# Cosformer attention with a quick-GELU feed-forward: the last block's stores issued by SyncE in place of GpSimd

## The chip, the cores and the metric

The kernel runs on one core of a Trainium2 chip. The metric is device time in microseconds (us) of one execution. Before the change the median of three runs is 294.02 us (294.0 to 294.31). The engines are named as in the profile: PE is TensorE's matmul, PEld its weight load, DVE is VectorE, ACT is ScalarE, POOL is GpSimd and SP is SyncE. A "q" behind an engine's name (SPq, POOLq) marks an instruction that its sequencer handles by itself: a semaphore wait, a drain, the issue of a transfer.

## The reference

Eight batches, eight heads, 576 positions, head size 64. A linear attention with cosine and sine weights gives an array of 4608 tokens by 512, and a feed-forward layer of width 2048 with the sigmoid form of GELU follows:

```python
q_p = phi(q, cos_w, sin_w)            # relu(x)*cos, relu(x)*sin, side by side
k_p = phi(k, cos_w, sin_w)
kv = np.einsum('bhsf,bhsd->bhfd', k_p, v)
num = np.einsum('bhsf,bhfd->bhsd', q_p, kv)
den = np.einsum('bhsf,bhf->bhs', q_p, np.sum(k_p, axis=2))[..., None] + 1e-06
x = (num / den).transpose(0, 2, 1, 3).reshape(4608, 512)
h = x @ w_in                          # 512 -> 2048
out = (h * (1.0 / (1.0 + np.exp(-1.702 * h)))) @ w_out   # 2048 -> 512, f32
```

## The kernel before

A block is one batch. Of its 576 tokens, 512 are worked on as four tiles of 128 (`t` = 0 to 3); the 64 that are left are a tail, and the tails of two batches make one more tile (`t` = 4). The order of the instructions is written out by hand, and every engine takes its own in that order.

In each block PE multiplies the block's x by `w_in` (`mm1`, L279), ACT applies the GELU (L284), and PE multiplies the result by `w_out` (`mm2`, L328). Between the parts of `mm2`, the attention of the next batch is done (L214, L227, and DVE at L235 to L239), and SP issues the transposing transfers that bring it into place (L268). The inputs of later blocks are loaded by transfers on SP's queue.

`mm2` is the function to follow. When the sum over the 16 pieces of `w_out` is complete, ACT copies the result from its accumulator into an SBUF tile `ysb` (L332; the pool has four such tiles), and for every piece of rows that `rows` names one transfer to `out` is issued (L335). In all blocks these stores are issued on POOL's queue, with one exception, the second half of the very last tile, which SP issues.

The last block (`b` = 7, `nb` is None) has no next batch to prepare. It does its `mm1`, then the first product of all tails that are left (`mm1_tails`, L307), then `mm2` for three tail tiles (two stores of 64 rows each), then `mm2` for the tiles 0 to 2 (one store of 128 rows each), and then the last tile in two halves of 256 columns, so that the final copy and the final store are small.

DMA completions are counted by semaphores. Each queue has eight that its transfers take in turn, and a transfer waits until the one before it on the same semaphore has landed. At the very end (the launch line, L538) SP waits for all of these semaphores, two to an instruction, in nine instructions. Then there is a barrier: every engine executes a drain instruction and then counts up one semaphore; POOL, after its own drain, waits for the four others and releases them all; POOL clears the semaphores; and the barrier is gone through a second time.

Of the kernel before, what the change touches and what calls it, by code (L numbers as in the profile page):

```python
# [19 lines left out]
def kernel(  # L20
# [9 lines left out]
    nc = tc.nc  # L30
    B, H, S, D = q.shape
    d_model = H * D
    d_ff = moe_w_in.shape[1]
    KC = d_model // 128
    FC = d_ff // 128
# [91 lines left out]
    def load_next(b):  # L127

        load_q(b, nc.sync)
        load(kf, k, b, nc.sync)  # L130
        load(vf, v, b, nc.sync)
# [14 lines left out]
    def trig(dst, src, j, act=False):  # L146
        i = src[:, :, ts(j, 64)]
        for cs, w in enumerate((cosw, sinw)):
            o = dst[:, j, :, ts(cs, 64)]
            if act:  # L150
                nc.scalar.activation(o, i, AF.Relu, scale=w[:, j:j + 1])
            else:
                nc.vector.tensor_scalar(o, i, 0.0, w[:, j:j + 1], op0=MAX, op1=MUL)  # L153

    def trig_q(c, act=False):
        n = 128 if c < 4 else 64
        if c < 4:
            i = qf[:, 0:2048].rearrange("p (h c d) -> p c h d", h=H, c=4)[:, c]
        else:
            i = qf[0:64, 2048:2560].rearrange("p (h d) -> p h d", h=H)  # L160
        for cs, w in enumerate((cosw, sinw)):
            o, sc = qn[0:n, c, :, ts(cs, 64)], w[0:n, NS + c:NS + c + 1]
            if act:
                nc.scalar.activation(o, i, AF.Relu, scale=sc)
            else:
                nc.vector.tensor_scalar(o, i, 0.0, sc, op0=MAX, op1=MUL)  # L166

    def vcopy(i0, i1, act=False):
        o = vt[:, :, i0:i1, 0:64].rearrange("p j i e -> p i j e")
        i = vf[:, i0:i1].rearrange("p i (j e) -> p i j e", e=64)  # L170
        if act:
            nc.scalar.activation(o, i, AF.Copy)
        else:
            nc.vector.tensor_copy(o, i)  # L174
# [19 lines left out]
    def qturn_dma(c):  # L194
        n = 128 if c < 4 else 64
        nc.sync.dma_start_transpose(out=qT[:, :, c * 128:c * 128 + n],
                                    in_=qn[0:n, c].rearrange("p h f -> p (h f)"))
# [3 lines left out]
    def kv_open(i0=0, i1=NI):  # L201
        t = pat.tile([128, 2, 512], F32, name="at")
        for i in range(i0, i1):
            st["kv", i] = t[:, :, ds((i - i0) * 65, 65)]
        st["ps", i0] = t[:, :, 0:(i1 - i0) * 65]
        if i0 == 0:
            st["kvs"] = small.tile([128, 2, NI, VW], BF16, name="kvs", bufs=2)

    def kv_mm(i0, i1, rhs, col, n):
        for i in range(i0, i1):  # L210
            for j in range(NS):
                for hh in range(2):
                    r = slice(hh * 64, hh * 64 + 64)
                    nc.tensor.matmul(st["kv", i][:, hh, ds(col, n)], kr[r, j, i, :], rhs(r, i, j),  # L214
                                     start=(j == 0), stop=(j == NS - 1))

    def kv_evac(i0, i1):
        o = st["kvs"][:, :, i0:i1, 0:65]
        nc.vector.tensor_copy(o, st["ps", i0].rearrange("p hh (i e) -> p hh i e", e=65))  # L219
# [3 lines left out]
    def num_mm(c):  # L223
        ps = pat.tile([128, 2, 512], F32, name="at")
        for h in range(H):
            i, hh = divmod(h, 2)
            nc.tensor.matmul(ps[:, h // 4, ds((h % 4) * 65, 65)], qT[:, h, ts(c, 128)],  # L227
                             st["kvs"][:, hh, i, 0:65], start=True, stop=True)
        nums[c] = [ps]

    def num_div(c):
        ps = nums[c][0]
        pv = ps[:, :, 0:260].rearrange("p a (h e) -> p a h e", h=4)
        den = small.tile([128, 2, 4], F32, name="den")
        nc.vector.tensor_scalar(den, pv[:, :, :, 64], 1e-6, None, op0=ADD)  # L235
        inv = small.tile([128, 2, 4], F32, name="inv")
        nc.vector.reciprocal(inv, den)  # L237
        xn = small.tile([128, 2, 4, 64], BF16, name="xn", bufs=4)
        nc.vector.tensor_tensor(xn, pv[:, :, :, 0:64],  # L239
                                inv.unsqueeze(3).to_broadcast([128, 2, 4, 64]), op=MUL)  # L240
        nums[c].append(xn)
# [3 lines left out]
    def x_open(b):  # L245
        x[b] = xpool.tile([128, KC, MT], BF16, name="xT")
# [40 lines left out]
    def mm1(b, fc):  # L287
        mm1_part(b, fc, 0, MT)
        gelu(fc)
# [6 lines left out]
    def mm1_tail_first(b, half):  # L296
        hps = pmm.tile([128, 8, 64], F32, name="mm")
        for f in range(8):
            for kc in range(KC):
                nc.tensor.matmul(hps[:, f], wcol(kc, half * 8 + f), xt[:, kc, ts(b, 64)],  # L300
                                 start=(kc == 0), stop=(kc == KC - 1))
        nc.scalar.activation(gt[:, ts(half, 8), ts(b, 64)], hps, AF.Gelu_apprx_sigmoid)

    def mm1_tails(fc):
        hps = pmm.tile([128, MT], F32, name="mm")
        for kc in range(KC):
            nc.tensor.matmul(hps[:, 128:B * 64], wcol(kc, fc), xt[:, kc, 128:B * 64],  # L307
                             start=(kc == 0), stop=(kc == KC - 1))
        nc.scalar.activation(gt[:, fc, 128:B * 64], hps[:, 128:B * 64], AF.Gelu_apprx_sigmoid)
# [4 lines left out]
    def rows(b, t):  # L314

        if t == 4:
            return [(64 * u, 64, out_j[NS - 1] if b + u == 1 else out[(b + u) * S - 64:(b + u) * S])
                    for u in range(2)]
        if b == 0:
            return [(64 * u, 64, out_j[2 * t + u]) for u in range(2)]  # L320
        return [(0, 128, out[b * S:b * S + 512].rearrange("(p c) d -> c p d", c=4)[t])]

    def mm2(b, t, lo, hi, c0=0, c1=d_model, last=False):
        if lo == 0:
            yp[b, t, c0] = pmm.tile([128, d_model], F32, name="mm")
        for fc in range(lo, hi):
            w = gT[fc][:, ts(t, 128)] if t < 4 else gt[:, fc, ts(b // 2, 128)]
            nc.tensor.matmul(yp[b, t, c0][:, c0:c1], w, w_out_sb[:, fc, c0:c1],  # L328
                             start=(fc == 0), stop=(fc == FC - 1))
        if hi == FC:  # L330
            ysb = ypool.tile([128, d_model], F32, name="ysb")
            nc.scalar.activation(ysb[:, c0:c1], yp[b, t, c0][:, c0:c1], AF.Identity)  # L332
            for p0, n, dst in rows(b, t):
                eng = nc.sync if last else nc.gpsimd
                eng.dma_start(out=dst[:, c0:c1], in_=ysb[p0:p0 + n, c0:c1])  # L335

    def idle(n, cols=512):
# [100 lines left out]
    for g in range(2):  # L438
        for t in range(4):
            mm2(0, t, 4 * g, 4 * g + 4)  # L440
    mm2(0, 0, 8, 12)
    mm2(0, 1, 8, 12)
    kv_open()
    kv_mm(0, 4, vt_rhs, 0, 65)
# [21 lines left out]
    for b in range(1, B):  # L466
        nb = b + 1 if b + 1 < B else None
        f0 = 5 if b == 1 else 0
        for fc in range(f0, FC):
            if nb is not None and fc == f0:  # L470
                for c in range(5):
                    trig_q(c)
                    qturn_dma(c)
            if nb is not None and fc == f0 + 1:
                for j in range(NS):
                    trig(kr, kf, j)
                vcopy(0, 4)
                if nb + 1 < B:
                    load_next(nb + 1)
            mm1(b, fc)  # L480
        if nb is not None:
            x_open(nb)
        if b == 1:
            mm1_tail_first(1, 0)
            mm1_tail_first(1, 1)
        if nb is not None:
            kv_open()
            kv_mm(0, 4, vt_rhs, 0, 65)
            kv_evac(0, 4)
        if b == 1:  # L490
            mm2(1, 4, 0, FC)
        if nb is None:
            for fc in range(FC):
                mm1_tails(fc)
            for u in range(3, B, 2):
                mm2(u, 4, 0, FC)
        for t in range(4):
            last = nb is None and t == 3
            if last:
                mm2(b, t, 0, FC, 0, 256)  # L500
                mm2(b, t, 0, FC, 256, 512, last=True)
                continue
            mm2(b, t, 0, 8)
            if nb is not None and t < 3:
                num_mm(2 * t)
                num_div(2 * t)
                xturn_dma(nb, 2 * t)
            mm2(b, t, 8, 16)
            if nb is not None and t < 2:
                num_mm(2 * t + 1)  # L510
                num_div(2 * t + 1)
                xturn_dma(nb, 2 * t + 1)
# [30 lines left out]
```

## Time and profile before

| What | us |
|---|---|
| median of three runs | 294.02 |
| the profiled execution's own time | 294.29 |
| its span, first to last instruction | 292.6 |
| PE busy | 284.0 (97%) |
| ACT busy / DVE busy / POOL busy | 128.7 / 123.6 / 57.5 |
| last matmul ends about | 287.5 |
| last copy into `ysb` (ACT) | 287.59 to 287.97 |
| last store, issued by SP | 288.0, landing 1.9 later |
| granted TensorE clock, mean | 0.998 |

The span is counted from the first instruction to the last one, and the execution's own time is 1.7 us longer. Starts are microseconds from the span's start. Where the profile gives "x3: 51/102/5292", those are the shortest, the median and the longest duration, in nanoseconds, of three instructions. "To landing" is the time from the issue of a transfer until its semaphore is counted up.

### The profile page before, as it was taken

What the parts mean: (1) busy time and instruction counts of PE and PEld (TensorE: products, weight loads), DVE (VectorE), ACT (ScalarE), POOL (GpSimd) and SP (SyncE); (2) the same over time, 40 slices, a digit from 0 to 9 for tenths busy, and PEclk for the clock granted to TensorE, in tenths of its full rate; (3) what the DMA queues carried; (4) which work ended last, traced back from release to release, by engine and by line L of the source; (5) the groups of instructions that cost most, each with busy time, mean ns of one, the idle gap of its engine ahead of it and who ended that gap; (6) DMA issues with size and microseconds to landing.
All of it is one profiled execution on the core that took longest, in us unless ns stands there. A gap on an engine that the chain in (4) does not pass through costs nothing.

```text
span 292.6 us, 6031 instructions
## 1 busy us (share of the span) xinstructions
PE 284.0 (97%) x2461; PEld 157.6 (54%) x2461; DVE 123.6 (42%) x355; ACT 128.7 (44%) x224; POOL 57.5 (20%) x70
## 2 busy tenths in 40 slices
PE   8979999999999999999999999999999999999993
PEld 3775646857545554555555554555455545564452
DVE  4774415881478047903691269225931510000000
ACT  7947733663116611562146304631464136771111
POOL 6350003200216001600061014201330110001211
PEclk9999999999999999999999999999999999999999
DMA  7999999999989964999598859895840430001311
GB/s 252 240 224 286 347 179 238 370 205 245 382 161 182 303 248 116 176 249 312 136 176 243 306 142 166 208 357 137 152 99 2 104 97 25 1 0 38 72 72 72
DMA packets 72731, 53.54 MB, mean 183 GB/s; under 512 B 52608, under 2 KB 62464, under 8 KB 72704
## 3 DMA queue, kind: packets, MB, share of 16 engines
q1 hardware_dynamic: 66160, 35.53, 49.6%
q0 software_dynamic: 6544, 17.63, 22.5%
q8 instruction: 19, 0.31, 0.4%
q14 instruction: 8, 0.07, 0.1%
HBM read 36.70 MB, written 9.44 MB: 158 GB/s over the span
## 4 chain that ended last, share of the span: by engine, by line
PE 93%; DMA 4%; DVE 1%; POOL 0%; issue 0%; ACT 0%; ACTq 0%
PE mm L328 43%; PE mm L279 38%; PE mm L307 4%; PE at L227 3%; PE at L214 3%; DMA vb<-in_v_dram 2%; PE mm L300 1%; DMA kf<-in_k_dram 1%; PE at L256 1%; DVE xn L239 1%; POOL vb L139 0%; DVE inv L237 0%; PE mm L182 0%; DVE den L235 0%; ACT ysb L332 0%
## 5 line engine op out<-in xcount | busy, mean ns | idle before, releaser
L328 PE MATMUL mm<-w_out_sb,g 128*128 128x512 bf16 (+1 forms) x528 | 117.4, 372 | 0.0
L279 PE MATMUL mm<-xT,w_in 128*128 128x512 bf16 (+1 forms) x608 | 113.5, 345 | 0.0
L284 ACT ACTIVATE g<-mm 128x512 bf16<-128x512 f32 x128 | 75.6, 598 | 32.0 <-PE mm L279 31.9
L335 POOL DMA_DIRECT2D out_dram<-ysb x44 | 46.4, 1057 | 216.8 <-ACT ysb L332 216.7
L279 PEld LDWEIGHTS <-w_in 128*128 128x128 bf16 x608 | 61.7, 113 | 49.1
L328 PEld LDWEIGHTS <-g 128*128 128x128 bf16 x528 | 48.8, 98 | 50.0
L332 ACT ACTIVATE ysb<-mm 128x512 f32<-128x512 f32 (+1 forms) x37 | 21.7, 586 | 115.8 <-PE mm L328 115.8
L219 DVE CAST kvs<-at 128x520 bf16<-128x520 f32 (+1 forms) x9 | 5.8, 642 | 56.4 <-PE at L214 56.4
L239 DVE TENSOR_TENSOR xn<-at,inv 128x512 bf16<-128x512 f32 x40 | 27.6, 691 | 1.4
L153 DVE TENSOR_SCALAR kr<-kf,cosw 128x256 bf16<-128x256 f32 x68 | 23.3, 343 | 9.1 <-DMA kf<-in_k_dram 9.1
L153 DVE TENSOR_SCALAR kr<-kf,sinw 128x256 bf16<-128x256 f32 x68 | 23.5, 346 | 0.0
L235 DVE TENSOR_SCALAR den<-at 128x8 f32<-128x8 f32 x40 | 6.6, 166 | 37.1 <-PE at L227 37.1
L227 PEld LDWEIGHTS <-qT 128*128 128x128 bf16 x320 | 14.5, 97 | 7.3
L166 DVE TENSOR_SCALAR qn<-qf,cosw 128x512 bf16<-128x512 f32 (+1 forms) x33 | 15.7, 477 | 3.8 <-DMA qf<-in_q_dram 3.8
L227 PE MATMUL at<-kvs,qT 128*128 128x65 bf16 x320 | 15.9, 193 | 0.0
L166 DVE TENSOR_SCALAR qn<-qf,sinw 128x512 bf16<-128x512 f32 (+1 forms) x33 | 15.8, 477 | 0.0
L328 PE MATMUL mm<-w_out_sb,gt 128*128 128x512 bf16 x64 | 14.2, 379 | 0.0
L214 PEld LDWEIGHTS <-kr 64*128 64x128 bf16 x648 | 10.3, 94 | 4.0 <-issue 3.1
L307 PE MATMUL mm<-xt,w_in 128*128 128x384 bf16 x64 | 10.6, 326 | 0.0
L328 PEld LDWEIGHTS <-gt 128*128 128x128 bf16 x64 | 6.2, 97 | 7.3
L174 DVE CAST vt<-vf 128x2304 bf16<-128x2304 f32 (+1 forms) x7 | 8.9, 1264 | 0.6 <-DMA vf<-in_v_dram 0.6
L307 PEld LDWEIGHTS <-w_in 128*128 128x128 bf16 x64 | 7.2, 113 | 3.3
(57 smaller groups left out, 101.5 us busy)
## 6 DMA issues: line engine op xcount, KB each, us to landing
kf<-in_k_dram SPq DMA_DIRECT2D x6, 1152.0 KB, 9.4
vf<-in_v_dram SPq DMA_DIRECT2D x6, 1152.0 KB, 12.3
out_dram<-ysb POOLq DMA_DIRECT2D x27, 256.0 KB, 2.7
qf<-in_q_dram SPq DMA_DIRECT2D x6, 1024.0 KB, 6.9
out_dram<-ysb POOLq DMA_DIRECT2D x17, 128.0 KB, 6.1
w_out_sb<-in_moe_w_out_dram POOLq DMA_DIRECT2D x4, 512.0 KB, 18.1
kf<-in_k_dram POOLq DMA_DIRECT2D x1, 1152.0 KB, 12.3
vf<-in_v_dram POOLq DMA_DIRECT2D x1, 1152.0 KB, 20.6
```

The costliest lines, as they stand in the source:

```text
L153: nc.vector.tensor_scalar(o, i, 0.0, w[:, j:j + 1], op0=MAX, op1=MUL)
L166: nc.vector.tensor_scalar(o, i, 0.0, sc, op0=MAX, op1=MUL)
L174: nc.vector.tensor_copy(o, i)
L214: nc.tensor.matmul(st["kv", i][:, hh, ds(col, n)], kr[r, j, i, :], rhs(r, i, j), start=(j == 0), stop=(j == NS - 1))
L227: nc.tensor.matmul(ps[:, h // 4, ds((h % 4) * 65, 65)], qT[:, h, ts(c, 128)], st["kvs"][:, hh, i, 0:65], start=True, stop=True)
L239: nc.vector.tensor_tensor(xn, pv[:, :, :, 0:64], inv.unsqueeze(3).to_broadcast([128, 2, 4, 64]), op=MUL)
L279: nc.tensor.matmul(hp[fc][:, t0:t1], wcol(kc, fc), x[b][:, kc, t0:t1], start=(kc == 0), stop=(kc == KC - 1))
L284: nc.scalar.activation(g, hp.pop(fc), AF.Gelu_apprx_sigmoid)
L307: nc.tensor.matmul(hps[:, 128:B * 64], wcol(kc, fc), xt[:, kc, 128:B * 64], start=(kc == 0), stop=(kc == KC - 1))
L328: nc.tensor.matmul(yp[b, t, c0][:, c0:c1], w, w_out_sb[:, fc, c0:c1], start=(fc == 0), stop=(fc == FC - 1))
L332: nc.scalar.activation(ysb[:, c0:c1], yp[b, t, c0][:, c0:c1], AF.Identity)
L335: eng.dma_start(out=dst[:, c0:c1], in_=ysb[p0:p0 + n, c0:c1])
```

## The change

All stores of the last block are issued by SP. The flag is renamed from `last` to `end`, and it is now given for the three tail tiles, for the tiles 0 to 2 and for both halves of tile 3. Ten stores go from POOL's queue to SP's: six of 64 rows by 512 columns, three of 128 by 512 and one of 128 by 256. The eleventh, the second half of tile 3, was on SP already. The two calls of `mm2` for each half of the sum are written as one in the last block, which leaves the order of the matmuls as it was. PE, DVE and ACT have the same instructions in the same order as before. SP has nothing else to issue in the last block: its last transposing transfer belongs to block 6. POOL's last store is now the one of block 6's tile 3.

```diff
-    def mm2(b, t, lo, hi, c0=0, c1=d_model, last=False):
+    def mm2(b, t, lo, hi, c0=0, c1=d_model, end=False):
...
-                eng = nc.sync if last else nc.gpsimd
+                eng = nc.sync if end else nc.gpsimd
                 eng.dma_start(out=dst[:, c0:c1], in_=ysb[p0:p0 + n, c0:c1])
...
             for u in range(3, B, 2):
-                mm2(u, 4, 0, FC)
+                mm2(u, 4, 0, FC, end=True)
         for t in range(4):
-            last = nb is None and t == 3
-            if last:
-                mm2(b, t, 0, FC, 0, 256)
-                mm2(b, t, 0, FC, 256, 512, last=True)
+            if nb is None:
+                for c in range(2 if t == 3 else 1):
+                    n = 256 if t == 3 else 512
+                    mm2(b, t, 0, FC, c * n, c * n + n, end=True)
                 continue
             mm2(b, t, 0, 8)
-            if nb is not None and t < 3:
+            if t < 3:
                 num_mm(2 * t)
                 num_div(2 * t)
                 xturn_dma(nb, 2 * t)
             mm2(b, t, 8, 16)
-            if nb is not None and t < 2:
+            if t < 2:
...
```

## The prediction

> **What bounds the kernel now.** I read the page first: the shares of the engines, then the chain that ended last.
>
> ```profile
> PE 284.0 (97%) x2461; PEld 157.6 (54%) x2461; DVE 123.6 (42%) x355; ACT 128.7 (44%) x224; POOL 57.5 (20%) x70
> ...
> PE 93%; DMA 4%; DVE 1%; POOL 0%; issue 0%; ACT 0%; ACTq 0%
> ```
>
> PE is busy from end to end, and a store is never what it waits for. So a change of store queues can matter only after the last matmul. The chain in order of time ends like this (start, length, what):
>
> ```profile
> 263.30 24.23 PE mm L328 x128
> 287.52 0.03 ACTq L332
> 287.55 0.04 issue
> 287.59 0.38 ACT ysb L332
> ```
>
> The chain stops at 287.97, but the span ends at 292.6: 4.6 us behind the last copy are not in it. Those 4.6 us are the place of this change, so next come the timeline of POOL's last stores, SP's one store, and then the end barrier's instructions (the launch line, L538), first all of POOL's, then SP's and POOL's in two short windows (288.38 to 288.8, and 289.85 to 290.2), then POOL's in a third (291.7 to 291.95).
>
> ```profile
> 284.99 0.54 POOL L335 DMA_DIRECT2D out_dram<-ysb  x1 [2.91 <-ACT ysb L332]
> 286.52 0.54 POOL L335 DMA_DIRECT2D out_dram<-ysb  x1 [0.99 <-ACT ysb L332]
> ```
>
> ```profile
> 288.00 0.36 SPq L335 DMA_DIRECT2D out_dram<-ysb  x1
> ```
>
> ```profile
> L538 POOLq EVENT_SEMAPHORE  x4: 17/17/17, 291.8 to 292.5; - x4
> L538 POOLq DRAIN  x3: 51/102/5292, 286.5 to 292.3; - x3
> ```
>
> ```profile
> L538 SPq EVENT_SEMAPHORE  x6: 28/28/28, 288.4 to 288.7; - x6
> ```
>
> ```profile
> L538 SPq EVENT_SEMAPHORE  x3: 28/28/28, 289.9 to 290.0; - x3
> L538 SPq DRAIN  x2: 7/10/13, 290.1 to 290.1; - x2
> L538 POOLq DRAIN  x1: 5292/5292/5292, 286.5 to 286.5; - x1
> ```
>
> ```profile
> L538 POOLq EVENT_SEMAPHORE  x2: 17/17/17, 291.8 to 291.9; - x2
> ```
>
> Two ends run side by side. SP issues the last store at 288.0, gets through six of its nine waits by 288.7, stands at the seventh until the store has landed (1.9 us after its issue, 289.9), and its drains are over at 290.1. POOL issues the store of the first half at 286.52, for 0.54 us, and then its drain, which the record shows from 286.5 for 5292 ns, so until 291.8. Only then does POOL look at the barrier, at 291.8. ACT and PE were done at 288.0. So for the last 1.7 us before 291.8 the only thing that is unfinished is POOL's drain: no transfer runs either (DMA share 0.00 from 289.4 on). From 291.8 the barrier, the clearing and the second barrier take 0.75 us, to 292.585 at the last instruction's end (292.5 and the rounding, with the span of 292.6).
>
> **The change part by part.**
>
> *Ten stores leave POOL.* That is six at about 0.53, three at about 0.55 and one at 0.54 us of POOL, 5.4 us in all, every one beside matmuls but the last. Their price in POOL's time is off the path, and I cost it at nothing: POOL stands idle 1 to 2.9 us before each tile's stores.
>
> *POOL's drain moves with them.* It comes directly behind POOL's last instruction, and after the change that is the store of block 6's tile 3, issued at about 240.06 and done at 240.6. What a POOL drain costs without a store just ahead of it is in the rows: 102 and 51 ns for the two others at the end, 181 ns for the one at the start, behind four memsets. The long one took 4.73 us from the end of the store ahead of it (287.07 to 291.8). Taken behind the store of 240.6 it would be over at about 245.3, with 45 us to spare, and POOL then waits at the barrier. If that cover were not there (a drain that lasts as long wherever it stands, and starts late), it would cost what it costs now. The bounds are therefore: all of 1.7 us gone, or nothing gone. I take the first, since the three short rows put the length down to the store ahead.
>
> The Trainium skill, page "VectorE: DVE Perf Modes", section "The DRAIN you can't avoid", says that the drains of the start and the end of a program are some 12 ns, constant, on all five engines. By that rule POOL's drain would be no matter at all, 292.6 would be set elsewhere and the sum would be zero. SP's rows, 7 to 13 ns, agree with it; POOL's 5292 ns does not, and the measurement decides.
>
> *Ten stores come to SP.* Issue on SP is 0.36 us (one row, 128 rows by 256 columns); I take 0.4 for all. The tail tiles give two stores each 3.45 us, 0.8 us of SP; the last two are 1.74 us apart (the two ACT copies, 285.85 and 287.59). SP has no other instruction between 236.3 and 288.0, and stands waiting 51.7 us for ACT, so nothing is queued behind these stores but the next store. At 288.0 SP has been free since about 286.6, so the last store is issued at the same time as now. Its packets ran from 288.8 to 289.4 in the window of that stretch; the store of the first half, issued at 286.26 (its copy ends 286.23) and with the same 1.9 us, has landed at 288.2, before those begin. Cost: 0. If the two did collide, the price is at most the 0.65 us in which the packets of one such store run.
>
> *The eight semaphores of SP's queue.* Each of the eleven stores first waits for the store or transpose eight places before it, 10 us or more earlier, against a landing of 1.9 to 2.7 us: nothing. ACT's wait for a free `ysb` tile (four tiles, three used in the 3.5 to 10 us between) is as far off; were a store to land in 8 us, it would begin to matter.
>
> *The order of SP's nine waits.* Before, the last store has the sixth of SP's eight semaphores, which stands in the seventh wait; two waits come behind it. After, the eleven stores take the semaphores from the sixth on, so the last has the eighth, in the ninth and last wait. The six waits at 288.4 to 288.7 are 0.06 us apart, so two fewer behind the landing are 0.12 us less. The landing at 289.88 then gives SP's drains at 290.02 in place of 290.14.
>
> *Sum, against the profiled execution.* SP arrives at the barrier at 290.02; POOL sees it 0.04 us later (the gap from the end of POOL's own drain to its wait, 291.80 to 291.84), and 0.75 us follow: the span ends at 290.81 in place of 292.59, 1.78 us less. The profiled execution would go from 294.29 to 292.51. It stands 0.27 us above the median of the runs; taking the same 1.78 us from the median of 294.02 gives 292.24 us. That the runs without a profile take nearly the same time as the profiled one says that the drain is no product of the profiling.
>
> **The rivals.**
>
> *A: the queue makes no difference at the end.* POOL's drain may not wait for POOL's store, but for everything that moves: it ends 1.9 us behind the landing of SP's store (289.9 to 291.8), and POOL's own store had landed at 288.6 (2.1 us after issue), 3.2 us before the drain ends. If the drain is held until the engines of both queues have been quiet for a while, it ends at 291.8 again; the nine waits of SP are then hidden, and the time is 294.02. Against it: the drain begins before SP's store exists, and nothing in a POOL instruction names SP's transfers. The Trainium skill, page "DMA: Bandwidth & Descriptors", section "Issuing engines are not separate DMA queues", holds that transfers from all engines run on the same 16 DMA engines and that the choice of issuer saves only issue time; by that rule, too, this change would leave the end as it is, since issue time is hidden here.
>
> *B: slower, the store of the first half holds up the last one on SP's queue.* Now both are on one queue. Break-even is where the last store lands 1.78 us later than now, 3.7 us after its issue; it decides for slower (by 0.2%, 0.59 us) from 4.3 us on. What speaks for it: transfers that stand in line on SP took long, the 128 KB parts of `qf` 7.4 us to landing at the median. If the first half's store took the 6.1 us that the page gives as median for 128 KB stores, it would land at 292.4, and a last store right behind it no sooner; with 0.14, 0.04 and 0.75 us the span ends at 293.3, 0.7 us later than now: 294.8 us. Against it: those transfers were issued behind up to 1152 KB each, while in the last block nothing else moves, and the same POOL stores there landed in 2.1 to 2.7 us, but for one in 3.8.
>
> *C: a part is given back.* A last store on a queue that has just been used lands in 2.7 us, the median of the 256 KB stores, in place of 1.9: 0.8 us less gain, 293.04 us.
>
> That the change does not move the stores is excluded: the built program has eleven stores on SP behind the last transpose, and POOL's list ends with block 6's.
>
> **How the numbers follow.** The forecast gets 0.76, its own range 292.0 to 292.6 (0.2 to 0.3 us each way, the spread of the runs shown); C 0.08; A 0.10; B 0.06. The predicted time is 292.24. The range takes in the forecast and C with the collision of 0.65 us and leaves out A and B, 0.16: 291.8 to 293.4. A measurement of this kernel tells about 0.2% from no change, 0.59 us: forecast and C are faster by more than that (1.78 and 0.98 us), A is the same, B is slower: 0.84, 0.10 and 0.06.
>
> **What would show it.** In the profile after: POOL's long drain starts at about 240 and not at 286.5, and the first barrier wait of POOL succeeds at about 290.06; SP's ninth wait, not its seventh, ends at the last landing; ACT and PE end at the same 287.97 and 287.5. A is right if a POOL drain still ends near 291.8 with SP done at 290. B or C is right if the last store's landing is over 1.9 us. The prediction is also wrong if the 1.7 us between the span and the execution's own time grow as the span shrinks.

## The result and the profile after

The changed kernel takes 292.24 us in the median (six runs, 292.08 to 292.69); six runs of the kernel before beside it give 294.29 us (294.0 to 294.35). The ratio is 0.9933, with a 95% interval of 0.9921 to 0.9946: 1.6 to 2.3 us faster. The profiled execution took 292.69 us, its span is 291.0 us, and the 1.7 us around the span are as before.

The chain of work of the changed kernel ends with these lines (start, length, what):

```profile
274.61 13.17 PE mm L328 x76
287.85 0.38 ACT ysb L332
```

Up to there nothing is gained; the last copy ends at 288.23, 0.25 us later than in the profile of before. That lies at the start of the program, far from the change, where PE waited for a load this time (timeline of PE; the brackets give the idle time and what ended it):

```profile
12.89 0.71 PE L214 MATMUL at<-vb,kr 64*128 64x64 bf16 x36 [0.44 <-DMA vb<-in_v_dram]
```

In the ten profiles of this study whose blocks run undisturbed the last copy starts between 287.19 and 288.90, whatever the end of the kernel looks like. So the profiles are compared from the end of the last copy on.

The end barrier of the changed kernel, first POOL's last store and the drain that stands behind it (in time a window from 240 to 245), then SP's waits before and at the landing, then POOL's barrier wait:

```profile
240.31 0.54 POOL L335 DMA_DIRECT2D out_dram<-ysb  x1 [2.91 <-ACT ysb L332]
```

```profile
L538 POOLq DRAIN  x1: 4538/4538/4538, 240.3 to 240.3; - x1
```

```profile
L538 SPq EVENT_SEMAPHORE  x8: 28/28/28, 288.6 to 289.1; - x8
```

```profile
L538 SPq DRAIN  x2: 7/10/13, 290.1 to 290.2; - x2
L538 SPq EVENT_SEMAPHORE  x1: 28/28/28, 290.1 to 290.1; - x1
```

```profile
L538 POOLq EVENT_SEMAPHORE  x2: 17/17/17, 290.2 to 290.3; - x2
```

POOL's long drain is over at 244.8 (240.29 and 4538 ns), beside the matmuls of block 7. Eight of SP's waits pass one behind the other and the ninth, 1.8 us after the issue of the last store, is the only one that holds; two drains follow, and POOL sees the barrier at 290.25, 0.03 us after SP. From the end of the last copy to the end of the span it was 4.61 us before (287.98 to 292.59) and is 2.76 us now (288.23 to 290.99): 1.84 us less. What ends last is now SP's store.

### The profile page after: what moved, and what is told of

The parts are those of the page before. It is cut to its first block, busy times and chain, and to the rows that moved or that the text cites. A ratio compares the mean times of both kernels' runs of the same rounds, so it can differ in the third digit from the quotient of the medians.

```text
span 291.0 us, 5997 instructions
## 1 busy us (share of the span) xinstructions
PE 282.5 (97%) x2427; PEld 157.7 (54%) x2461; DVE 123.9 (43%) x355; ACT 128.6 (44%) x224; POOL 52.9 (18%) x60
## 3 DMA queue, kind: packets, MB, share of 16 engines
q0 software_dynamic: 5968, 15.93, 20.3%
## 4 chain that ended last, share of the span: by engine, by line
PE 91%; DMA 4%; ACT 1%; DVE 1%; issue 1%; POOL 0%; ACTq 0%
PE mm L328 43%; PE mm L279 36%; PE mm L307 4%; PE at L227 3%; PE at L214 3%; DMA vb<-in_v_dram 3%; PE mm L300 2%; ACT g L284 1%; DMA kf<-in_k_dram 1%; PE at L256 1%; DVE xn L239 1%; POOL vb L139 0%; DVE inv L237 0%; PE mm L182 0%; DVE den L235 0%
## 5 line engine op out<-in xcount | busy, mean ns | idle before, releaser
L328 PE MATMUL mm<-w_out_sb,g 128*128 128x512 bf16 (+1 forms) x507 | 116.0, 373 | 1.2 <-issue 0.2
L335 POOL DMA_DIRECT2D out_dram<-ysb x34 | 42.0, 1236 | 174.9 <-ACT ysb L332 174.8
L153 DVE TENSOR_SCALAR kr<-kf,cosw 128x256 bf16<-128x256 f32 x68 | 23.9, 352 | 9.5 <-DMA kf<-in_k_dram 9.5
```

## The experiments

The prediction gave a reason: the drain is long because of the store just ahead of it. Ten stores were moved, and only one of them should matter. The first four kernels test that.

**One store moved.** In the kernel before, the store of the last tile's first half goes to SP:

```diff
-                mm2(b, t, 0, FC, 0, 256)
+                mm2(b, t, 0, FC, 0, 256, last=True)
```

> The kernel before with one store moved: that of the last tile's first half goes to SP, the other nine stay on POOL. Theory (POOL's drain ends 4.0 to 4.7 us after the end of POOL's last store, the two lengths seen so far): POOL's last store is now that of tile 2, 284.99 to 285.53, the drain ends at 289.5 to 290.3, SP is done at about 290.1, and nearly the whole gain is there: 1.5 to 1.8 us faster than before, 292.5 to 292.8. Rival A (the drain waits until the transfers of both queues have been quiet for about 1.9 us): no gain, 294.3. Rival that the number of stores on POOL counts: nine of ten stay, so about a tenth of the gain, 294.1.

292.47 us against 294.06 us, ratio 0.9945 (0.9928 to 0.9963). POOL's last store and its drain in this kernel:

```profile
284.68 0.54 POOL L335 DMA_DIRECT2D out_dram<-ysb  x1 [2.91 <-ACT ysb L332]
```

```profile
L538 POOLq EVENT_SEMAPHORE  x2: 17/17/17, 289.9 to 290.0; - x2
L538 POOLq DRAIN  x1: 5209/5209/5209, 284.7 to 284.7; - x1
```

The drain ends 4.65 us behind the store, at 289.86, about when SP is done (289.74). The one store carries nearly the whole gain; the other nine are not needed for it. Neither rival's time came, 294.3 for the quiet stretch or 294.1 for the number of stores.

**All but that store moved.** In the changed kernel the store of the first half goes back to POOL:

```diff
-                    mm2(b, t, 0, FC, c * n, c * n + n, end=True)
+                    mm2(b, t, 0, FC, c * n, c * n + n, end=t < 3 or c == 1)
```

> The changed kernel with one store put back on POOL: that of the last tile's first half; the other nine stay on SP. Theory: this one store gives back the gain, since the drain again stands behind a store that ends at 287.07. If the length is 4.73 us as before, the drain ends at 291.8 and the time is that of before, 294.3; if a store with no others close ahead of it leaves only the 3.98 us that the changed kernel showed behind block 6's, it ends at 291.05 and the time is about 293.5. Rival that the number of stores on POOL counts: nine tenths of the gain are kept, about 292.4.

293.39 us against 294.06 us, ratio 0.9984 (0.9967 to 1.0001). Nine moved stores without the tenth bring 0.5 us of 294 by this ratio (0.7 between the medians), with an interval from nothing to 1.0. The drain is shorter than before, though, 3.99 us behind the store in place of 4.73, which is the second length that the theory allowed, at about 293.5:

```profile
287.83 0.54 POOL L335 DMA_DIRECT2D out_dram<-ysb  x1 [45.93 <-ACT ysb L332]
```

```profile
L538 POOLq DRAIN  x1: 4556/4556/4556, 287.8 to 287.8; - x1
L538 POOLq EVENT_SEMAPHORE  x1: 17/17/17, 292.4 to 292.4; - x1
```

**All stores on POOL.** In the kernel before, the last store of all goes to POOL too:

```diff
-                mm2(b, t, 0, FC, 256, 512, last=True)
+                mm2(b, t, 0, FC, 256, 512)
```

> The kernel before with the opposite change: the one store that SP issued, of the last tile's second half, goes to POOL too. Theory: POOL's last store is at 288.0 to 288.55, and the drain ends 4.0 to 4.7 us later, 292.5 to 293.3, in place of 291.8: 0.7 to 1.5 us slower than before, 295.0 to 295.8. Rival A (quiet for 1.9 us after the last landing, here at 290.1): about 292.0, 0.2 us slower than before, 294.5.

295.86 us against 294.06 us, ratio 1.0061 (1.0042 to 1.008). The store is issued at 287.94 for 0.54 us and the drain ends at 293.29, 4.81 us behind it:

```profile
287.94 0.54 POOL L335 DMA_DIRECT2D out_dram<-ysb  x1 [1.21 <-ACT ysb L332]
```

```profile
L538 POOLq DRAIN  x1: 5372/5372/5372, 287.9 to 287.9; - x1
L538 POOLq EVENT_SEMAPHORE  x1: 17/17/17, 293.3 to 293.3; - x1
```

The last transfer of the program had landed at 290.05 (SP's wait for it ends at 290.07), 3.2 us earlier and not 1.9; in the changed kernel the drain was over 45 us before the last landing. So the drain does not wait for a quiet stretch of all queues. That rival falls.

**A POOL instruction at the end.** The changed kernel, and behind ACT's last copy POOL copies one element. Its drain then stands at the end of the program, but 48 us behind POOL's last store:

```diff
                 eng.dma_start(out=dst[:, c0:c1], in_=ysb[p0:p0 + n, c0:c1])
+            if b == B - 1 and t == 3 and c0 == 256:
+                nc.gpsimd.tensor_copy(gate[0:1, 2:3], ysb[0:1, 256:257])
```

> The changed kernel with one more POOL instruction: after the last copy of ACT, POOL copies one element of the last ysb tile (about 0.18 us, at 288.2), so that its drain comes 48 us after POOL's last store but at the end of the program. Theory (what is long is the work behind the store, over long before): the drain is short, 0.2 us or less, is done by 288.6, and the time is that of the changed kernel, 292.2 to 292.4. Rival D (the first drain of POOL after any store takes 4 to 5 us whenever it comes): it ends at 292.4 to 293.4, later than before's 291.8, and the time is 294.9 to 295.9.

294.43 us against 294.06 us, ratio 1.0012 (0.9997 to 1.0027): the whole gain is gone. POOL's timeline and its drain:

```profile
287.63 0.17 POOL L337 COPY gate<-ysb 1x1 f32<-1x1 f32 x1 [47.44 <-ACT ysb L332]
```

```profile
L540 POOLq DRAIN  x1: 4122/4122/4122, 287.6 to 287.6; - x1
L540 POOLq EVENT_SEMAPHORE  x1: 17/17/17, 291.8 to 291.8; - x1
```

The drain takes 3.93 us behind a copy of 0.17 us, with no store for 48 us. My theory falls here: the length does not come from the store ahead, and the work is not over long before. It is spent in the drain itself, whenever that comes. Rival D comes nearer, but its 4 to 5 us and 294.9 are more than was measured.

**What sets the length.** The kernels so far differ in how many transfers POOL issues in the whole program, and the drain's time behind the instruction ahead of it follows this number closely: 58 transfers 4.81 us, 57 (before) 4.73, 56 4.65, 48 3.99, 47 (after) 3.98 and 3.93. From 56 to 58 the steps of one are 0.08 us; from 47 to 48 it is 0.01 or 0.06, where the two at 47 lie 0.05 apart. The next kernels test that as theory E, against the rival that the length is a constant.

*A drain in the middle.* The kernel before, all stores left where they were, and one drain more on POOL behind block 6:

```diff
+        if b == B - 2:
+            nc.gpsimd.drain()
```

> The kernel before (ten stores of the last block on POOL) with one drain instruction more on POOL, behind block 6's last store. Theory E (a drain of POOL takes about 0.083 us for each transfer that POOL has issued since its last drain; so far 57 transfers gave 4.73 us behind the instruction ahead, 56 gave 4.65, 58 gave 4.81, 48 gave 3.99, 47 gave 3.98 and 3.93): the drain in the middle takes about 3.9 us beside block 7's matmuls, the one at the end stands for ten stores only, 0.8 us, and is over at about 287.9, before SP. Nearly the full gain with the stores left where they were: 292.2 to 292.6. Rival F (the length is a constant of the first drain at the program's end, 4 to 4.8 us): no gain, 294.1.

292.41 us against 294.03 us, ratio 0.9943 (0.993 to 0.9956): about the same gain, with no store moved. The two drains of this kernel, from its lines 514 (the new one) and 540 (the end):

```profile
L514 POOLq DRAIN  x1: 4542/4542/4542, 239.7 to 239.7; - x1
```

```profile
286.23 0.54 POOL L335 DMA_DIRECT2D out_dram<-ysb  x1 [0.99 <-ACT ysb L332]
```

```profile
L540 POOLq DRAIN  x1: 2604/2604/2604, 286.2 to 286.2; - x1
```

The first pays 3.98 us for 47 transfers. The second, behind a store of 286.23 to 286.77, has ten to pay and ends at 288.81, 2.04 us behind the store: over before SP, but longer than the 0.9 us that ten should take.

*Forty loads more.* The changed kernel with the copy at the end, and forty small loads on POOL after block 0:

```diff
+    extra = one.tile([128, 40, 8], F32, name="extra")
+    for n in range(40):
+        nc.gpsimd.dma_start(out=extra[:, n], in_=q[0, 0, 0:128, 0:8])
```

> The changed kernel with POOL's copy of one element at the end, as in the run with that copy alone, and with forty small loads (128 rows of 32 bytes, into a tile that nobody reads) issued on POOL after block 0. Theory E: 87 transfers, a drain of 7.2 us behind the copy, 3.3 us more than with 47: 297.7. Rival F (constant): 294.4, as with the copy alone. If packets or bytes count and not transfers: forty loads move 0.16 MB in 5120 rows of 32 bytes, beside 16 MB on POOL's queue, so by bytes 294.5.

The time, 310.27 us (298.87 to 313.36), missed the 297.7 and says nothing of the drain: stores of block 1 stand behind the loads on POOL, ACT waits 9.4 us for a free `ysb` tile until 94.7, and then PE waits for ACT. The drain itself can be read. It takes 7.20 us behind the copy of 295.30 to 295.47, where theory E gave 7.2 and a constant 3.9:

```profile
295.30 0.17 POOL L337 COPY gate<-ysb 1x1 f32<-1x1 f32 x1 [47.44 <-ACT ysb L332]
```

```profile
L544 POOLq DRAIN  x1: 7389/7389/7389, 295.3 to 295.3; - x1
L544 POOLq EVENT_SEMAPHORE  x1: 17/17/17, 302.7 to 302.7; - x1
```

The forty loads moved 1% of the bytes of POOL's queue, so bytes are not what counts. Packets, the pieces in which the profile lists a transfer, are not either: the queue's rose from 5968 to 7248, and in that proportion the 3.93 us would have become 4.8. It is the number of transfers that counts.

*No stores on POOL.* The changed kernel with the copy at the end, and all stores of all blocks on SP; POOL is left with 13 loads:

```diff
-                eng = nc.sync if end else nc.gpsimd
+                eng = nc.sync
```

> The changed kernel with POOL's copy of one element at the end, and with all stores of all blocks on SP, so that POOL issues only its 13 loads, the last one at about 23. Theory E: a drain of about 1.1 us behind the copy at 287.8, over before SP is done: 292.2 to 292.5, unless the stores on SP hold up a load or a transpose in the blocks before. Rival F (constant): 294.4.

292.73 us against 294.03 us, ratio 0.9964 (0.995 to 0.9978). The drain ends at 289.34, 1.15 us behind the copy, before SP is done:

```profile
288.02 0.17 POOL L337 COPY gate<-ysb 1x1 f32<-1x1 f32 x1 [263.94 <-ACT ysb L332]
```

```profile
L540 POOLq DRAIN  x1: 1346/1346/1346, 288.0 to 288.0; - x1
```

The time is 0.2 us above the range expected. SP's list of waits alone makes more than that, 0.37 us against the changed kernel: with another number of stores the last one has another of the eight semaphores, its wait is the third of nine, and from 289.81, where it passes, to the end of SP's drains (290.31) it takes 0.51 us; in the changed kernel, where it is the ninth, 0.14.

*Copy and middle drain.* The kernel with the copy at the end and the drain behind block 6, so that no transfer lies between the two drains. Against the kernel with the copy at the end:

```diff
+        if b == B - 2:
+            nc.gpsimd.drain()
```

> The kernel with POOL's copy of one element at the end (the changed kernel and that copy, 294.4), with one drain more on POOL behind block 6's last store. Theory E (0.082 us for each transfer since POOL's last drain, and 0.09): no transfer is issued between the two drains, so the one at the end takes 0.1 to 0.2 us where it took 3.93, and the time is that of the changed kernel, 292.2 to 292.5. If a drain starts the count anew only in part (ten stores behind a drain took 2.04 us in place of the 0.9 that the sum gives), it takes over 1 us; if the middle drain had no part in that gain, 3.9 us and 294.4.

Three runs took 292.19, 292.2 and 292.48 us against 294.01 us, ratio 0.9938 (0.9918 to 0.9958). A fourth took 1118 us, which nothing here explains; the ratio leaves it out. The drain at the end ends 0.07 us behind the copy (288.07 to 288.24), where it ended 3.93 us behind it without the middle one:

```profile
288.07 0.17 POOL L337 COPY gate<-ysb 1x1 f32<-1x1 f32 x1 [47.44 <-ACT ysb L332]
```

```profile
L542 POOLq DRAIN  x1: 267/267/267, 288.1 to 288.1; - x1
```

With no transfer between the two drains, the count was wholly gone.

*Nine stores behind a drain.* The kernel with one store moved, and the drain behind block 6. Against the kernel before:

```diff
-                mm2(b, t, 0, FC, 0, 256)
+                mm2(b, t, 0, FC, 0, 256, last=True)
...
+        if b == B - 2:
+            nc.gpsimd.drain()
```

> The kernel before with the first half's store on SP (nine stores of the last block on POOL) and one drain more on POOL behind block 6's last store: a look at what makes up the 2.04 us that ten stores behind a drain took. Theory E alone: 0.83 us behind the end of tile 2's store. If a drain also can't end before the last store of POOL has landed (2.6 us after its issue, 256 KB; with ten stores it ended 0.48 us behind that landing), about 2.5 us behind the store's end. Either way over before SP is done: 292.2 to 292.6.

One run, 293.1 us, above the range expected; its last copy starts late, at 288.16 (287.59 before), so only the drain is read. It ends 2.49 us behind the end of the store (285.56 to 286.10), at 288.58:

```profile
L540 POOLq DRAIN  x1: 3049/3049/3049, 285.5 to 285.5; - x1
```

With the 2.6 us that such a store of 256 KB takes to land in the profile with one store moved, the landing is at 288.16, 0.4 us before the drain's end; in the kernel with ten stores behind a drain it was 0.5 us (286.23 and 2.1 us to land, 288.33, against 288.81). A drain thus seems to wait for POOL's own last landing as well. Two profiles fit that, and neither takes the landing apart from the rest, so it is not shown.

All the other long drains, and the one with no transfer, lie on one line; the two with nine and ten transfers, 2.49 and 2.04 us, lie above it and are left out. The table sets the measured time behind the instruction ahead against 0.09 us and 0.0817 us for each transfer since POOL's last drain, the line through the kernels with 13 and 87:

| transfers | kernel | measured us | line us |
|---|---|---|---|
| 0 | copy and middle drain | 0.07 | 0.09 |
| 13 | no stores on POOL | 1.15 | 1.15 |
| 47 | copy at the end; changed kernel | 3.93; 3.98 | 3.93 |
| 48 | all but one moved | 3.99 | 4.01 |
| 56 | one moved | 4.65 | 4.67 |
| 57 | before | 4.73 | 4.75 |
| 58 | all on POOL | 4.81 | 4.83 |
| 87 | forty loads more | 7.20 | 7.20 |

POOL's other instructions do not count: POOL has 13 of them before (70 in the profile, less 57 transfers), which at 0.08 us each would be 1.1 us, and the line's constant is 0.09.

None of these versions beats the changed kernel. Once POOL's drain is out of the way, SP's last store ends last, and a still shorter drain has nothing to win.

## Why the prediction was right, point by point

**What bounds the end.** Right. The 1.7 us between SP's arrival and POOL's were nearly all that there was to gain (the order of the waits gave 0.12), and PE's and ACT's work did not move.

**POOL's drain moves with its stores.** Right in place, and over long before the end: forecast from 240.6 to 245.3, measured from 240.85 to 244.83. Its length was taken at 4.73 us as before and measured 3.98, since POOL had issued ten transfers fewer. The reason behind it was wrong. That "the three short rows put the length down to the store ahead" is the step that failed: those rows fit a drain with no transfer to count (0.07 us in the kernel with copy and middle drain), and the store ahead has no part in it. The copy at the end showed that, and 0.08 us for each transfer took its place. The number came out all the same, and in that there is luck: the drain stands behind POOL's last instruction, which moved to 46 us earlier, and by either reason the drain is then over long before the end. The kernel with the copy at the end, where the reasons differ, was expected at 292.2 to 292.4 by the same reason and took 294.43.

**Ten stores at nothing each on POOL and on SP.** Right for the time. The issue on SP, taken at 0.4 us, was 0.33 to 0.59 us, and 0.59 for the second store of a tail tile. It stays hidden.

**The last store behind another on SP's queue.** Taken at 0, and so it was: 1.82 us from issue to the wait's end in place of 1.87. Rivals B (held up by the first half's store) and C (2.7 us) did not occur. The upper end of the range, 293.4, had room for C (293.04) or for the collision of 0.65 us (292.89), but not for both at once (293.69).

**The order of the nine waits.** Right: from the end of the last store's wait to the end of the drains it took 0.26 us before (289.88 to 290.14) and 0.14 now (290.08 to 290.22), 0.12 less as forecast. The kernel without POOL stores shows the same term with the other sign.

**The sum.** 1.78 us, measured from the end of the last copy 1.84. The rest is the landing, 0.05 us quicker, and a hundredth in the barrier. The profile's span fell by 1.59 only, since that profile's start cost 0.25 us more. Between the medians it is 2.05 us, with an interval that holds 1.78. The 292.24 that was forecast started from 294.02, and the six runs of before have 294.29: that the median meets it to the hundredth is chance.

**Rival A.** It got 0.10, and the kernel with all stores on POOL excludes it. The rule that was set beside it, in the Trainium skill, page "DMA: Bandwidth & Descriptors", section "Issuing engines are not separate DMA queues", that the issuer only changes issue time, does not hold for the end of this program: one store's issuer made 1.6 us. The Trainium skill's rule of constant drains of some 12 ns (page "VectorE: DVE Perf Modes", section "The DRAIN you can't avoid") held for SP (7 to 13 ns) and not for POOL. The page speaks of drains that the runtime adds, and the rows here stand at the kernel's launch line, so they may not be the same.

## What to carry to other kernels

Read what lies behind the last instruction of the chain: the end barrier has rows of its own, and an engine's drain there can be the longest thing in the program's tail. Where the issuing queue has a drain that grows with its transfers, either let that queue finish early or drain it once in the middle, where other work covers it; here both bring about the same (ratios 0.9933 and 0.9943, with overlapping intervals). And a number that comes out right does not vouch for the reason: the cheapest test of "the work behind the store" was to put something else behind the store.

## What the runs showed of the hardware

POOL's drain took 0.082 us for each transfer that POOL had issued since its last drain, 0.07 us with none and 7.20 us with 87, though the transfers had landed long before (246 us before, in the kernel with 13). Behind nine and ten transfers, the last of them just issued, it took 2.49 and 2.04 us, longer than that sum. An extra drain in the middle set the count to nothing. SP's drains took 7 to 13 ns in all eleven profiles, with 93 to 138 transfers issued on SP. The profile lists POOL's transfers under a queue of its own kind (`software_dynamic`, 6544 packets before) and SP's under another (`hardware_dynamic`, 66160); whether that is why POOL's drain counts them no run here shows. Nor does any trace show what the engine does in that time.
